# A convolution and feed-forward kernel: the conv one unit later in its block, and the softmax of a batch in four pieces

## The chip, the cores and the metric

The kernel runs on one core of one Trainium2 chip. The metric is device time in microseconds (us), from start to end of the program on that core. A core has several engines that run side by side and wait for each other by semaphores: TensorE (PE in the profile, with its weight loads shown as PEld), VectorE (DVE), ScalarE (ACT), GpSimd (POOL), and SyncE (SP), which here only issues DMA transfers.

## What is computed

Two stages follow each other. The first is a convolution whose weights come from a softmax: for each of 8 batches, 4096 positions and 8 heads, 7 numbers are turned into weights, and these weigh the last 7 positions of `x`. The second is a feed-forward layer with a squared ReLU on each of the 32768 positions.

```python
# x: (8, 4096, 192), weight_gen: (8, 4096, 8, 7), w_in: (192, 2048), w_out: (2048, 192)
w = np.exp(weight_gen - max over the 7)
w = w / (sum over the 7 + 1e-09)
x_pad = six zero rows ahead of x in each batch
out[b, s, h] = sum over k of w[b, s, h, k] * x_pad[b, s + k, h]      # 24 channels a head
h = np.maximum(out.reshape(32768, 192) @ w_in, 0.0)
result = (h * h) @ w_out
```

## The kernel before

The work is cut into 33 blocks. Blocks 0 and 1 hold 512 positions each, all others two sub-blocks of 512. A batch is 8 sub-blocks, so batch 3 begins with block 13 and each later batch four blocks after the one before it.

In each block the program issues 16 units (`u`, the first product with `w_in`), eight half quarters (`M`, the second product of the block before), and one conv (`C`), which makes the input of the next block. Softmax pieces are put in ahead of chosen units. The order from block 7 on:

```python
steady_spread = "MuMuuu" * 2 + "MCuMuuu" + "MuMuuu"
```

A unit: three pairs of matmuls into an `h` buffer of PSUM (a pool of three, which the conv shares), a ReLU on ACT into `t1`, and for two units together the square on DVE into `g`.

```python
def st_unit(j, u):
    h = ps_h.tile([P, 2, TB], f32, name="h", tag="h")     # ps_h: 3 buffers
    ...        # three pairs of 64-row matmuls, 512 columns: L518
    nc.scalar.activation(out=t1[:, e], in_=h, func=ActF.Relu)             # L532
    ...
    nc.vector.tensor_tensor(out=g[...], in0=t1[...], in1=t1[...], op=AluOp.mult)   # L536
```

A quarter of the second product is two half quarters: the first needs `g` of units 0 to 7 of the block before, the second that of units 8 to 15. Its result is summed by ACT and DVE.

```python
def quarters():
    ...
        st_mm2(j, qt, FCS[0], (0, 1), o)      # 32 matmuls, 64 rows, 192 columns: L560
        yield
        st_mm2(j, qt, FCS[1], (0, 1), o)
        o_sum(j, qt, (0, 1), o)               # ACT copy L574, then DVE add L576
        ...
        yield
```

The conv reads two bands, one for each sub-block, that DVE makes in the same block ahead of units 1 and 5 from the softmax weights. Its matmuls alternate between the two sub-blocks. The first two columns of heads are done into one `h` buffer, the other two into a second; ACT casts the first and DVE the second.

```python
def st_band(j, tiles):
    nc.vector.tensor_tensor(out=bd_t[j][...], in0=wr_t[j][...], in1=mask[...], op=AluOp.mult)  # L381

def st_conv_spread(j):
    for ks in ((NK, NK - 1), (0, 1)):
        yp = ps_h.tile([P, 2, TB], f32, name="yp", tag="h")
        for k in ks:
            for i in range(NT):
                for half in (0, 1):           # the two sub-blocks
                    for e in (0, 1):
                        nc.tensor.matmul(out=yp[p0 : p0 + 32, k - k0, a:b],
                                         lhsT=x_t[s][...], rhs=bd[...], ...)       # L450
        copy = nc.vector.tensor_copy if k0 == 0 else nc.scalar.copy
        copy(out=y[:, k0 : k0 + 2], in_=yp)                                        # L460
    ...        # four DMA moves inside y, from SyncE
```

The softmax of a batch works on 32 rows a partition and 6 of halo (batch 2: two parts of 16 and 6). A piece is a range of these rows: the exponential on ACT, then, at its place in the plan, on DVE a sum, a reciprocal, and products into `v_big`, four to each run of rows inside a group of 8. After the last piece the weights go to DRAM, and from there the rows of each sub-block are loaded for its band.

```python
def soft(s):
    lo, hi = next(s.softs)
    s.total(lo, hi)                    # DVE reduction L257
    s.recip(lo, hi)                    # DVE reciprocal L264
    s.scale(lo, hi, nc.vector)         # DVE products L272, four per run of rows
    if hi < s.rh:
        return
    ...
        s.store(nc.sync)               # vd<-v_big, L286
        stored.add(s)
        for w in [w for w in waiting if w[0] is s]:
            waiting.remove(w)
            load_rows(w[1])            # wr<-vd, lines 323 to 333
```

For each block j the program calls `load_rows(j + 2)` at the start; if the store has not been issued by then, the loads are issued right behind it.

```python
PIECE = 8
TIMES = {
    ...
    (2, 1): ((7, 9), (7, 13), (8, 9)),                       # (block, unit) of each piece
    (3, 0): ((9, 9), (9, 13), (10, 9), (10, 13), (11, 0)),
}
...
times = TIMES.get((b, k)) or (
    (f - 6, 9), (f - 5, 9), (f - 4, 9), (f - 3, 9), (f - 3, 13)   # f: the batch's first block
)
```

Of the kernel before, what the change touches and what calls it, by code (L numbers as in the profile page):

```python
# [9 lines left out]
def kernel(  # L10
# [49 lines left out]
    R = S // P  # L60
    HALO = KK - 1
# [37 lines left out]
    FIRST = 8  # L99
# [495 lines left out]
    with nc.allow_low_precision("fp16 matmul pipeline"), tc.manual_schedule():  # L595

        block_of = {n: j for j, (s, c) in enumerate(BLOCKS) for n in range(s, s + c)}
        parts = []
# [65 lines left out]


        steady = "MuMuuu" * 3 + "MuuuMCu"
        steady_spread = "MuMuuu" * 2 + "MCuMuuu" + "MuMuuu"
        plans = {
            0: "B1 X1 u u u E1 S1 u C u u u u",
            1: "L3 u u B2 M E2 B3 u M E2 u u S2 u M u C u S2 M",  # L670
# [8 lines left out]
        def at(j, u, kind, *args):  # L679
            fill.setdefault((j, u), []).append((kind, *args))  # L680

        PIECE = 8

        TIMES = {
            (1, 0): ((3, 15), (4, 0)),
            (1, 1): ((4, 15), (5, 0)),
            (1, 2): ((4, 2), (5, 1), (5, 15)),
            (2, 0): ((6, 1), (6, 15), (7, 0)),
            (2, 1): ((7, 9), (7, 13), (8, 9)),
            (3, 0): ((9, 9), (9, 13), (10, 9), (10, 13), (11, 0)),  # L690
        }

        def exp_time(j, u):

            if u == 0:
                return j - 1, 12
            return j, {1: 0, 2: 1, 7: 3, 8: 4, 9: 4, 13: 12, 15: 8}[u]

        for n, s in enumerate(parts):
            piece = s.rh if n < 2 else PIECE  # L700
            s.pieces = [(lo, min(lo + piece, s.rh)) for lo in range(0, s.rh, piece)]
            s.exps = iter(s.pieces)
            s.softs = iter(s.pieces)
        for n, s in enumerate(parts[4:], 4):
            b, f = s.b, s.fb
            k = n - min(m for m, p in enumerate(parts) if p.b == b)
            times = TIMES.get((b, k)) or (
                (f - 6, 9), (f - 5, 9), (f - 4, 9), (f - 3, 9), (f - 3, 13)
            )
            assert len(times) == len(s.pieces)  # L710
            for j, u in times:
                at(*exp_time(j, u), "E", n)
                at(j, u, "S", n)
            at(times[0][0] - 1, 0, "L", n)
# [65 lines left out]
        for j in range(NBLK):  # L780
# [3 lines left out]
            for step in plans[j].split():  # L784
                kind, n = step[0], int(step[1:] or 0)
# [73 lines left out]
```

## Time and profile before

| | us |
|---|---|
| median of 3 runs | 743.38 |
| lowest and highest | 742.02, 743.45 |
| span of the profiled execution | 740.5 |
| TensorE busy | 730.4 |
| DVE busy | 626.1 |
| ACT busy | 617.1 |

"Busy" is the time in which at least one instruction of an engine is shown as running. Matmuls overlap, and the profile works out their ends, so a busy TensorE need not be one at its peak. A line of the timeline has the start, the length, the engine, the line of the kernel, the operation, what it writes and reads, the number of instructions merged into it, and, in brackets, how long the engine was idle before and what ended this. A line of the table of windows has the stretch, its length, the busy time and number of instructions of each engine, the clock granted to TensorE, and the share and rate of the DMA engines. The largest groups by line of the kernel, with busy time in us and the mean of one in ns:

```profile
L532 ACT ACTIVATE t<-h 128x1024 f16<-128x1024 f32 x512 | 496.2, 1025 | 53.3 <-PE h L518 52.9
...
L536 DVE TENSOR_TENSOR g<-t 128x2048 f16<-128x2048 f16 (+1 forms) x309 | 308.5, 1036 | 26.9 <-ACT t L532 26.6
...
L381 DVE TENSOR_TENSOR bd<-wr,mask 128x4160 f16<-128x4160 f16 (+3 forms) x89 | 149.3, 1702 | 4.9 <-DMA wr<-v_first 4.9
```

### The profile page before, as it was taken

To read this page: it belongs to the slowest core of one execution; us is meant where nothing else is said; L and a number is where in the kernel's file an instruction comes from. 1 tells how busy PE (TensorE), PEld (TensorE's weight loads), DVE (VectorE), ACT (ScalarE), POOL (GpSimd) and SP (SyncE) were. 2 spreads that over 40 slices of the span, in tenths; PEclk is the share of its full clock that TensorE was granted. 3 is DMA by queue.
4 is the path that set the end of the run, shared out by engine and by line. 5 is a ranking of instruction groups with operands and counts; after the bars stand their busy time and mean duration, and the time that the engine had idled before them with its cause. 6 is when DMAs were issued, how large, how long until landed. Compare 5 with 4: busy or idle time off the path is not lost. (4 is left out here: it accounts for less than half of the span.)

```text
span 740.5 us, 31100 instructions
## 1 busy us (share of the span) xinstructions
PE 730.4 (99%) x14106; PEld 531.9 (72%) x14106; DVE 626.1 (85%) x824; ACT 617.1 (83%) x730; POOL 100.1 (14%) x148
## 2 busy tenths in 40 slices
PE   7999999999999999999999999999999999999998
PEld 3767777877777777777777777777777777777777
DVE  4999898999899988889888889889889887778853
ACT  4998888988888888888888888888888888888883
POOL 7322222321001100011000110010100110001000
PEclk9999999999999999999999999999999999999999
DMA  7845444794454432545335444353444334444012
GB/s 206 131 82 135 80 68 106 145 156 116 96 126 77 93 74 66 123 105 95 56 69 130 92 86 81 62 126 100 65 87 80 62 85 81 66 86 76 29 45 66
DMA packets 126544, 68.71 MB, mean 93 GB/s; under 512 B 85193, under 2 KB 122636, under 8 KB 125900
## 3 DMA queue, kind: packets, MB, share of 16 engines
q1 hardware_dynamic: 80908, 48.12, 22.8%
q0 software_dynamic: 45360, 18.50, 21.5%
q8 instruction: 110, 1.80, 1.0%
q14 instruction: 22, 0.18, 0.1%
q10 hardware_dynamic: 144, 0.10, 0.0%
HBM read 50.18 MB, written 28.70 MB: 107 GB/s over the span
## 5 line engine op out<-in xcount | busy, mean ns | idle before, releaser
L532 ACT ACTIVATE t<-h 128x1024 f16<-128x1024 f32 x512 | 496.2, 1025 | 53.3 <-PE h L518 52.9
L560 PEld LDWEIGHTS <-g 64*128 64x128 f16 (+1 forms) x8032 | 344.3, 94 | 62.8 <-DVE g L536 3.5
L560 PE MATMUL o<-w_o,g 64*128 64x192 f16 (+1 forms) x8032 | 380.7, 243 | 1.1 <-DVE g L536 0.8
L536 DVE TENSOR_TENSOR g<-t 128x2048 f16<-128x2048 f16 (+1 forms) x309 | 308.5, 1036 | 26.9 <-ACT t L532 26.6
L518 PE MATMUL h<-y,w_p 64*128 64x512 f16 x2400 | 291.9, 376 | 0.0
L518 PEld LDWEIGHTS <-w_p 64*128 64x128 f16 x2400 | 112.7, 94 | 96.4
L381 DVE TENSOR_TENSOR bd<-wr,mask 128x4160 f16<-128x4160 f16 (+3 forms) x89 | 149.3, 1702 | 4.9 <-DMA wr<-v_first 4.9
L576 DVE TENSOR_TENSOR o_sb<-o,o_sb 128x384 f32<-128x384 f32 x123 | 68.4, 556 | 68.8 <-ACT o_sb L574 68.1
L333 POOL DMA_DIRECT2D xt<-in_x_dram x62 | 52.1, 844 | 426.8 <-PE yp L450 366.7
L574 ACT COPY o_sb<-o 128x384 f32<-128x384 f32 x129 | 61.5, 477 | 44.3 <-PE o L560 44.3
L518 PE MATMUL h<-y,w_i 64*128 64x512 f16 (+1 forms) x768 | 82.2, 350 | 1.8 <-ACT t L532 0.8
L518 PEld LDWEIGHTS <-w_i 64*128 64x128 f16 x768 | 37.2, 94 | 27.7 <-issue 4.0
L460 ACT CAST y<-yp 128x1024 f16<-128x1024 f32 x25 | 25.3, 1012 | 12.3 <-PE yp L450 12.3
L450 PE MATMUL yp<-bd,xt 128*32 128x104 f16 (+1 forms) x2000 | 31.8, 210 | 0.1
L460 DVE CAST y<-yp 128x1024 f16<-128x1024 f32 x25 | 30.4, 1216 | 0.0
L450 PEld LDWEIGHTS <-xt 128*32 128x32 f16 x2000 | 26.1, 95 | 5.9 <-issue 4.2
L272 DVE TENSOR_TENSOR v_big<-ex,rcp 128x112 f16<-128x112 f32 (+1 forms) x136 | 27.3, 263 | 2.5 <-DMA vd<-v_big 1.3
L250 ACT ACTIVATE ex<-wg 128x448 f32<-128x448 f32 (+2 forms) x44 | 27.0, 617 | 1.8 <-DMA wg<-in_weight_gen_dram 1.8
L257 DVE TENSOR_REDUCE ssum<-ex 128x64 f32<-128x448 f32 (+2 forms) x44 | 26.1, 594 | 2.3 <-ACT ex L250 2.3
L264 DVE RECIPROCAL rcp<-ssum 128x64 f32<-128x64 f32 (+2 forms) x44 | 23.7, 539 | 1.5
L323 POOL DMA_DIRECT2D xt<-in_x_dram x7 | 3.9, 553 | 126.2 <-PE yp L450 90.3
L363 POOL DMA_DIRECT2D wr<-v_first x31 | 16.9, 564 | 16.0 <-DVE v_first L272 15.8
(34 smaller groups left out, 95.4 us busy)
## 6 DMA issues: line engine op xcount, KB each, us to landing
out_dram<-o_sb SPq DMA_DIRECT2D x63, 384.0 KB
xt<-in_x_dram POOLq DMA_DIRECT2D x42, 240.0 KB, 4.7
wg<-in_weight_gen_dram SPq DMA_DIRECT2D x4, 1064.0 KB
xt<-in_x_dram POOLq DMA_DIRECT2D x20, 192.0 KB, 4.9
wr<-vd SPq DMA_DIRECT2D x38, 80.0 KB
vd<-v_big SPq DMA_DIRECT2D x5, 512.0 KB
y<-y SPq DMA_DIRECT2D x100, 24.0 KB
wg<-in_weight_gen_dram SPq DMA_DIRECT2D x5, 392.0 KB
```

The lines of the kernel that those rows point to most:

```text
L250: nc.scalar.activation(out=self.ex[:, lo:hi].rearrange("p r g k e -> p (r g) k e"), in_=self.wg[:, lo:hi].rearrange("p r (g e) k -> p (r g ...
L272: eng.tensor_tensor(out=bass.AP(tensor=v.tensor, offset=v.offset + lo * H * SL + lo % SL * 2 + g * SL * 2, ap=[list(v.ap[0]), [H * SL + 2, ...
L333: eng.dma_start(out=dst[:, first:last], in_=ap)
L381: nc.vector.tensor_tensor(out=bd_t[j][:, H * lo : H * (lo + len(tiles) * n)].rearrange("p (g m c) -> p g m c", g=shape[1], c=2 * SL), in0= ...
L450: nc.tensor.matmul(out=yp[p0 : p0 + 32, k - k0, a:b], lhsT=x_t[s][:, i, c0 : c0 + 32], rhs=bd[:, head // 2, e, 0 : b - a], start=True, sto ...
L460: copy(out=y[:, k0 : k0 + 2], in_=yp)
L518: nc.tensor.matmul(out=h[:, half, jj * th : (jj + 1) * th], lhsT=w_in_chunk(w, u * per + jj, slot, half), rhs=y_t[j][r0 : r0 + RT, k, 0:th ...
L532: nc.scalar.activation(out=t1[:, e], in_=h, func=ActF.Relu)
L536: nc.vector.tensor_tensor(out=g[:, a : e + 1], in0=t1[:, a : e + 1], in1=t1[:, a : e + 1], op=AluOp.mult)
L560: nc.tensor.matmul(out=oo[:, cc * Dm : (cc + 1) * Dm], lhsT=g[r0 : r0 + n, cc * P : (cc + 1) * P], rhs=w_o[r0 : r0 + n, fc, :], start=(fc ...
L574: nc.scalar.copy(out=o_sb, in_=o[0][:, c])
L576: nc.vector.tensor_tensor(out=o_sb, in0=o[1][:, c], in1=o_sb, op=AluOp.add)
```

## The change

It has two parts. In the plan of blocks 7 and later the conv moves behind unit 8; its bands, its inputs and its results stay as they are. And the softmax of a batch of 32 rows is cut into four pieces (8, 10, 10 and 10 rows) instead of five (8, 8, 8, 8 and 6). From batch 4 on these stand one to a block, in the blocks 5, 4, 3 and 2 ahead of the batch's first one, where before they stood in the blocks 6 to 3 ahead with two in the last. Batch 3 is handled alike except for its first two pieces, which still share block 9, and the second part of batch 2 has two pieces of 11 rows instead of three. What it is for: the band has more time to be ready ahead of the conv, and DVE and ACT have no block with two pieces of softmax.

```diff
-        steady_spread = "MuMuuu" * 2 + "MCuMuuu" + "MuMuuu"
+        steady_spread = "MuMuuu" * 2 + "MuCMuuu" + "MuMuuu"
...
-        PIECE = 8
+        CUTS = {FIRST: (0, 8, FIRST + HALO), R // 2: (0, 8, 16, R // 2 + HALO), R: (0, 8, 18, 28, R + HALO)}
+        CUTS_FOR = {(2, 1): (0, 11, R // 2 + HALO)}
...
-            (2, 1): ((7, 9), (7, 13), (8, 9)),
-            (3, 0): ((9, 9), (9, 13), (10, 9), (10, 13), (11, 0)),
+            (2, 1): ((7, 9), (8, 9)),
+            (3, 0): ((9, 9), (9, 13), (10, 9), (11, 9)),
...
-            piece = s.rh if n < 2 else PIECE
-            s.pieces = [(lo, min(lo + piece, s.rh)) for lo in range(0, s.rh, piece)]
+            k = n - min(m for m, p in enumerate(parts) if p.b == s.b)
+            cuts = (0, s.rh) if n < 2 else CUTS_FOR.get((s.b, k), CUTS[s.r])
+            s.pieces = list(zip(cuts, cuts[1:]))
...
-                (f - 6, 9), (f - 5, 9), (f - 4, 9), (f - 3, 9), (f - 3, 13)
+                (f - 5, 9), (f - 4, 9), (f - 3, 9), (f - 2, 9)
```

## The prediction

> **What bounds the kernel now.** I read the page first, then the weight loads in order of time, then DVE and SyncE around one conv. The page's busy line:
>
> ```profile
> PE 730.4 (99%) x14106; PEld 531.9 (72%) x14106; DVE 626.1 (85%) x824; ACT 617.1 (83%) x730; POOL 100.1 (14%) x148
> ...
> PEclk9999999999999999999999999999999999999999
> ```
>
> TensorE is hardly ever idle and its clock is never cut, so time falls only where its stream pauses. From block 7 on the stream is periodic, and each block holds one conv. The time from one conv's first weight load to the next, cut into windows with DVE's busy time:
>
> ```profile
> 203.67:226.36 22.69, 20.83 (x29) 1.00 0.52 119
> 226.36:249.20 22.84, 21.84 (x36) 1.00 0.42 88
> ...
> 316.19:338.70 22.51, 20.45 (x30) 1.00 0.44 95
> 338.70:360.82 22.12, 19.17 (x24) 1.00 0.40 72
> 360.82:383.11 22.29, 19.07 (x23) 1.00 0.39 71
> ```
>
> The second number is the length. I call 22.11 us the clean period. Most blocks take 22.27, those with two softmax pieces 22.5 to 22.8. There are two pauses to explain.
>
> Pause one, inside the conv. The weight loads of two convs, each cut off about 0.31 us after its first load:
>
> ```profile
> 316.19 0.41 PEld L450 LDWEIGHTS <-xt 128*32 128x32 f16 x17 [0.16 <-issue]
> ```
>
> ```profile
> 695.23 0.40 PEld L450 LDWEIGHTS <-xt 128*32 128x32 f16 x29 [0.16 <-issue]
> ```
>
> 17 loads against 29 in the same time. In the first, the third of 80 matmuls starts 0.19 us after the first; it is the first to read the band of the second sub-block, and DVE ends that band late:
>
> ```profile
> 314.01 2.31 DVE L381 TENSOR_TENSOR bd<-wr,mask 128x4160 f16<-128x4160 f16 x1
> ```
>
> It ends at 316.32, 0.14 us after the conv's first load. So an ordinary conv's loads take 1.15 to 1.19 us, an undisturbed one's 0.99 to 1.02. The latter come where the last sub-block of a batch is next: its band is cut in two and only the last matmuls need the second part. Of the 25 convs of this form 7 are undisturbed, 17 lose 0.16 us, and one (at 249.20, after a softmax piece at the top of the block) takes 1.34 us and loses 0.35.
>
> Pause two, at the top of the block after one with two pieces:
>
> ```profile
> 329.94 0.11 PEld L560 LDWEIGHTS <-g 64*128 64x128 f16 x4 [0.30 <-DVE g L536]
> ```
>
> The second softmax piece, ahead of unit 13, makes DVE late with the last squares (g), which the second half quarter of the next block needs.
>
> **What the Trainium skill says.** "Perfetto Trace Analysis", Tensor Engine Instruction: the profile's end of a matmul is computed, not observed. The trace agrees: L560 has a mean of 243 ns, but its pairs start 83 ns apart. I therefore count starts. "TensorE: Matmul & The Clock Gate", The mechanism: a weight load passes running matmuls only if its row group differs. Agrees: before a conv, whose loads take all 128 rows, the load queue idles 0.16 us. "VectorE: DVE Perf Modes", The TRN2 errata: a fixed cost for each instruction. Agrees: L272 starts every 207 ns at 112 elements (4 in 0.83 us) and every 178 ns at 84 (4 in 0.71), so 1.07 ns an element and 88 ns fixed. "DMA: Bandwidth & Descriptors", Anatomy of one DMA: the fixed share, mostly completion, is about 2 us. No run here separates it; below I use measured times from store to load.
>
> **Part one: the conv one unit later.** Nothing is added or removed; M, C, u8, M becomes M, u8, C, M. In starts of first matmuls, before: M to conv 1.42 us, conv to u8 1.24 (1.09 undisturbed), u8 to M 0.66, M to u9 1.32: 4.64, or 4.48 undisturbed. After: M to u8 1.32 (as elsewhere, 306.28 to 307.60). From a 512-column unit to a conv there is one pair in the early part, 53.59 to 54.34, so 0.75. Conv to M 1.09, M to u9 1.32. Sum 4.48. So the order itself costs nothing, and the gain is the wait for the band: the conv now starts about 0.65 us later, 0.5 us after the band has ended. 17 x 0.16 + 0.35 = 3.1 us.
>
> Buffers: three h buffers rotate. After the change u9 takes u8's, u10 the first conv half's, u11 the second's. DVE's cast of the second half ends at 319.74 as now (DVE is busy until 318.5 anyway). u10, which needs it today, starts near 319.95; u11, which will, near 320.5. That slack grows.
>
> **Part two: four pieces.** Per batch of 32 rows plus halo, DVE loses one reduction and one reciprocal; with cuts off the multiples of 8, 20 products become 28 shorter ones. From the groups by form: a reduction of 448 elements 609 ns, of 336 493, so 1.04 ns an element; a reciprocal of 64 552, of 48 453, so 6.2 ns each. A 10-row piece: reduction 0.73 + reciprocal 0.65 + four products of 8 rows 0.83 + four of 2 rows 4 x (88 + 28 x 1.07 ns) = 0.47, about 2.6 us with gaps, against 2.0 for 8 rows. Four pieces 9.8 us, five today 9.7 (four of 2.0 and a last of 1.65). DVE's sum stays; its spread changes: one piece a block. What goes:
> - Batches 4 to 7: the piece at unit 13 in blocks 14, 18, 22, 26. 22.52 - 22.27 = 0.25 each, 1.0 us.
> - Block 7: from the window 158.72 to 181.41, 22.69, whose conv is undisturbed: 22.69 - 22.11 = 0.58 gone.
> - Block 10: 22.84 - 22.27 = 0.57 gone.
> - Block 9 keeps both its pieces, and the second grows from 8 to 10 rows. Its excess is 22.69 - 22.11 = 0.58 and should grow by about 0.5.
> Sum 1.0 + 0.58 + 0.57 - 0.5 = 1.6 us.
>
> Do longer pieces at unit 9 delay anything? After an 8-row piece DVE idles 0.42 us before the next o_sum, and TensorE writes that bank again 0.67 us after the sum's end at 325.91. So 0.6 us more delays the sum 0.2 and TensorE not at all; even the 11-row pieces of batch 2 (0.85 more) use up less than this.
>
> **Part three: the later store.** The last piece moves from block f-3, unit 13, to f-2, unit 9, so the chain store, load, band gets short:
>
> ```profile
> SPq L323 <- DMA vd<-v_big: 20.9, 6, 5.8
> ```
>
> ```profile
> 327.58 0.35 SPq L286 DMA_DIRECT2D vd<-v_big  x1
> 332.62 0.33 SPq L323 DMA_DIRECT2D wr<-vd  x1
> 333.00 0.98 SPq L333 DMA_DIRECT2D wr<-vd  x2
> ```
>
> From store to first load 5.0 us here, 2.65 at the shortest (416.77 to 419.42); the loads' packets run until 335.4, 2.8 us more. After the change, put into this block's time, the piece ends near 323.2, the store goes at 323.3, the loads at 326 to 328.3 and land at 329 to 331.1. The band that reads them is now at 331.30 (308.78 + 22.3 gives 331.1). It just fits; an unlucky store makes DVE late by some tenths. Five batches, at 0.1 us each: +0.4.
>
> **Sum.** 743.4 - 3.1 - 1.6 + 0.4 = 739.1 us.
>
> **Rivals.**
> - The conv after a unit costs more. For it: in the early part the load queue idles 0.42 us before such a conv, against 0.16 after a half quarter. Times 25 the difference is 6.5 us: 745. Against it: the load queue runs ahead of the matmuls there, and starts of matmuls show 0.75 from unit to conv, of which the unit takes 0.66. I give it one in ten.
> - The late load becomes the wait. For it: the 5.0 us above and one wait of 5.8. A band late by 1 us eats DVE's slack, then delays o_sum and the second band; I put half a microsecond of it on TensorE, for 5 batches 2.5 us: 741 to 742. Against it: three of the stores took under 3 us. Two in ten.
> - DVE was the hidden bound and takes back what the conv gives. DVE's 19.1 us in a period of 22.1 speaks against it, as do its idle times before o_sum. It would leave 742 to 743. One in ten.
>
> **Range and chances.** Everything that this change can move is the sum of the pauses, about 6 us after block 7, 0.8% of the time. So 2% either way (14.9 us) is out of reach unless something new waits in every block. Low end 736.8: all pauses gone, and block 9 no worse. High end 742: half the gain lost to late loads. Chances: same 0.98, 0.01 each for faster and slower.
>
> **What would show it.** The conv's weight loads at 0.99 to 1.02 us in all 25; periods of 22.10 to 22.15, except one near 23.2 after block 9; no wait of L560 for g at the tops of blocks 8, 11, 15, 19, 23 and 27; about 5 DVE waits for wr from vd, if any, each below 0.5 us. I am wrong on part one if the loads become short but the periods stay at 22.27, and on part three if L381 idles by a microsecond for DMA.

## The result and the profile after

| | before | after |
|---|---|---|
| median, us | 741.74 | 736.27 |
| lowest and highest | 740.44, 743.45 | 735.19, 737.00 |
| span of the profiled execution | 740.5 | 734.8 |

The ratio of after to before is 0.9921, with a 95% interval of 0.9904 to 0.9937: 0.8% faster, or some 5.9 us by the ratio and 5.5 by the medians. The prediction said 739.1 us, with 736.8 as its low end, so the kernel came out 0.5 us below the whole range. The median of before stands 1.6 us below the 743.38 that the prediction started from.

The page's busy line after the change:

```profile
PE 725.9 (99%) x14106; PEld 529.4 (72%) x14106; DVE 627.3 (85%) x856; ACT 613.5 (83%) x724; POOL 100.2 (14%) x148
```

It looks like the old one: TensorE at 99%, DVE at 85%. A reader who stops at shares of busy time sees no difference between the kernels; the difference is in TensorE's pauses, and those show in the time from one conv to the next. The table of windows after the change, with DVE's busy time:

```profile
203.10:226.38 23.28, 21.45 (x33) 1.00 0.37 69
226.38:248.46 22.08, 19.59 (x28) 1.00 0.49 114
314.71:336.80 22.09, 19.59 (x28) 1.00 0.48 115
336.80:358.89 22.09, 19.69 (x28) 1.00 0.50 104
358.89:380.97 22.08, 19.08 (x23) 1.00 0.40 73
```

All 24 periods from the conv in block 7 to the one in block 31 now take 22.07 to 22.12 us, but for the first line here, which holds the second half of block 9 and the top of block 10. From the first of these convs to the last it was 536.5 us before (158.72 to 695.23) and is 531.3 now (158.93 to 690.24): 5.2 us gained. The spans differ by 5.7 us. The other 0.5 us lie ahead of block 7, where nothing on TensorE was changed (taken up at the end); to see it one must count from the half quarter ahead of the first conv, since the conv itself now stands 0.65 us later in its block.

One conv of the kernel after, cut off about 0.31 us after its first weight load:

```profile
314.71 0.40 PEld L450 LDWEIGHTS <-xt 128*32 128x32 f16 x30 [0.42 <-issue]
```

30 loads in the time in which 17 were done before. The instructions around the same conv:

```profile
311.89 2.32 DVE L381 TENSOR_TENSOR bd<-wr,mask 128x4160 f16<-128x4160 f16 x1
...
312.65 1.48 PE L560 MATMUL o<-w_o,g 64*128 64x192 f16 x32
...
313.97 0.81 PE L518 MATMUL h<-y,w_p 64*128 64x512 f16 x6
...
314.71 0.98 PEld L450 LDWEIGHTS <-xt 128*32 128x32 f16 x80 [0.42 <-issue]
```

The band ends at 314.21, 0.50 us ahead of the conv. The load queue's idle time ahead of a conv has grown from 0.16 to 0.42 us, and the conv nevertheless costs no more: from M at 312.65 over u8 at 313.97, the conv at 314.71 and the next M at 315.77 to u9 at 317.10 it takes 4.45 us in starts of matmuls, where the prediction worked out 4.48 and the kernel before took 4.64.

The pause that is left, at the top of block 10, in three parts:

```profile
215.76 0.28 PEld L560 LDWEIGHTS <-g 64*128 64x128 f16 x8 [0.54 <-DVE g L536]
216.37 0.12 PEld L560 LDWEIGHTS <-g 64*128 64x128 f16 x4 [0.32 <-DVE g L536]
216.97 0.11 PEld L560 LDWEIGHTS <-g 64*128 64x128 f16 x4 [0.49 <-DVE g L536]
```

No other block from 7 to 32 waits for g; one wait at 723.3, behind the last block, was there before too (728.9). And the store, its loads, and the bands that read them, for the batch that begins with block 17 (SyncE's lines, then DVE's):

```profile
343.08 0.34 SPq L286 DMA_DIRECT2D vd<-v_big  x1
346.09 0.34 SPq L323 DMA_DIRECT2D wr<-vd  x1
346.48 0.97 SPq L333 DMA_DIRECT2D wr<-vd  x2
```

```profile
350.37 0.56 DVE L576 TENSOR_TENSOR o_sb<-o,o_sb 128x384 f32<-128x384 f32 x1 [1.51 <-ACT o_sb L574]
350.84 2.38 DVE L381 TENSOR_TENSOR bd<-wr,mask 128x832 f16<-128x832 f16 x2
```

The bands start with no idle time before them, 3.4 us after the last load was issued. From store to first load it takes 3.0 us here, and 3.0 to 3.8 for the five batches.

### The profile page after: what moved, and what is told of

It reads as the page before. It is cut to its first block, busy times and chain, and to the rows that moved or that the text cites. A ratio compares the mean times of both kernels' runs of the same rounds, so it can differ in the third digit from the quotient of the medians.

```text
span 734.8 us, 31124 instructions
## 1 busy us (share of the span) xinstructions
PE 725.9 (99%) x14106; PEld 529.4 (72%) x14106; DVE 627.3 (85%) x856; ACT 613.5 (83%) x724; POOL 100.2 (14%) x148
## 4 chain that ended last, share of the span: by engine, by line
PE 70%; DVE 0%; ACT 0%; issue 0%
PE o L560 35%; PE h L518 32%; PE yp L450 3%; DVE g L536 0%; ACT o_sb L574 0%
## 5 line engine op out<-in xcount | busy, mean ns | idle before, releaser
L450 PEld LDWEIGHTS <-xt 128*32 128x32 f16 x2000 | 24.4, 95 | 10.6 <-issue 10.6
L272 DVE TENSOR_TENSOR v_big<-ex,rcp 128x112 f16<-128x112 f32 (+5 forms) x180 | 29.9, 237 | 2.1 <-DMA vd<-v_big 1.1
L450 PE MATMUL yp<-bd,xt 128*32 128x104 f16 (+1 forms) x2000 | 28.3, 209 | 0.0
L250 ACT ACTIVATE ex<-wg 128x560 f32<-128x560 f32 (+4 forms) x38 | 25.9, 682 | 1.7 <-DMA wg<-in_weight_gen_dram 1.7
L257 DVE TENSOR_REDUCE ssum<-ex 128x80 f32<-128x560 f32 (+4 forms) x38 | 25.3, 666 | 2.2 <-ACT ex L250 2.2
L264 DVE RECIPROCAL rcp<-ssum 128x80 f32<-128x80 f32 (+4 forms) x38 | 22.8, 600 | 1.3
```

Source lines behind the costliest of these rows:

```text
L250: nc.scalar.activation(out=self.ex[:, lo:hi].rearrange("p r g k e -> p (r g) k e"), in_=self.wg[:, lo:hi].rearrange("p r (g e) k -> p (r g ...
L272: eng.tensor_tensor(out=bass.AP(tensor=v.tensor, offset=v.offset + lo * H * SL + lo % SL * 2 + g * SL * 2, ap=[list(v.ap[0]), [H * SL + 2, ...
L450: nc.tensor.matmul(out=yp[p0 : p0 + 32, k - k0, a:b], lhsT=x_t[s][:, i, c0 : c0 + 32], rhs=bd[:, head // 2, e, 0 : b - a], start=True, sto ...
```

## The experiments

**The conv alone.**

```diff
-        steady_spread = "MuMuuu" * 2 + "MCuMuuu" + "MuMuuu"      # kernel before
+        steady_spread = "MuMuuu" * 2 + "MuCMuuu" + "MuMuuu"
```

> Only the conv moved behind unit 8; softmax pieces as before. Theory (conv waits for the second band): the 25 convs' weight loads all take 0.96 to 1.00 us, ordinary periods fall from 22.27 to 22.09, and the pauses at the tops of blocks 8, 10, 11, 15, 19, 23 and 27 stay: 17 x 0.18 + 0.35 + 7 x 0.02 = 3.5 us less than before, 738.2 us against 741.7. Rival (the gain of the change is the softmax's, one piece a block, and the conv's place only matters together with it): less than 1 us gained, 740.8 or more.

Measured: 738.36 us against 741.63, ratio 0.9952 (0.9940 to 0.9965). The loads of all 25 convs take 0.96 to 1.00 us; ordinary periods are 22.07 to 22.11; the periods that had a pause of the second kind keep it, at 22.66, 22.69, 22.67 and four of 22.33 to 22.36. Such a pause, at the top of block 15:

```profile
328.62 0.11 PEld L560 LDWEIGHTS <-g 64*128 64x128 f16 x4 [0.30 <-DVE g L536]
```

From the first conv to the last it takes 532.9 us, 3.6 less than before. The theory holds, and its rival, that the conv's place matters only together with the softmax, does not.

**The softmax alone.**

```diff
-        steady_spread = "MuMuuu" * 2 + "MuCMuuu" + "MuMuuu"      # kernel after
+        steady_spread = "MuMuuu" * 2 + "MCuMuuu" + "MuMuuu"
```

> Only the softmax in four pieces; the conv stays ahead of unit 8. Theory: the pauses at the tops of blocks 8, 11, 15, 19, 23 and 27 go (0.58 + 0.57 + 4 x 0.25 = 2.15 us), the one at the top of block 10 grows by 0.6 us, ordinary periods stay at 22.27: 1.6 us less than before, 740.1 us against 741.7. Rival (softmax is the main part): 3 us or more gained, 738.7 or less.

Measured: 739.44 us, ratio 0.9972 (0.9961 to 0.9983), 2.2 us less than before. Ordinary periods stay at 22.25 to 22.30, the third matmul of 17 convs still starts 0.19 us after the first, the period after the conv of block 9 grows to 23.30, and the other pauses for g are gone. From the first conv to the last it takes 534.6 us, 1.9 less than before. Against this the sum of 1.6 was 0.3 us too small for one reason: the conv at 249.20, which lost 0.35 us to the band, lost it because a softmax piece stood at the top of that block. Taking the piece away mends it too (its loads take 1.00 us), so either part alone brings the 0.35 that the prediction put under the conv.

The two gains, 0.48% and 0.28%, add up to 0.76%, with that 0.35 us in both; the change as a whole brings 0.79%. Each of the three is known to some 0.1 to 0.2%, so the parts do not need each other.

**The band in two operations, the conv where it was.**

```diff
         last = NT - int(tile_start(j, NT - 1) != starts[-1])     # kernel before
+        if j % 2 and j >= BLOCKS[FIRST_SPREAD][0]:
+            last = NT - 1
```

> The kernel before, conv and softmax untouched, but the second band of each block from 8 on is made in two operations (tiles 0 to 3, then tile 4), as it is already at the end of a batch; 18 DVE operations more. Theory (the conv's third matmul waits for the second band): the first part ends about 0.4 us earlier, the conv's loads take 0.99 to 1.02 us everywhere, and the time falls by 17 x 0.16 + 0.35 = 3.0 us, to about 738.7, without moving the conv. Rival (the conv's move gains by more slack in the three h buffers and in the casts): nothing gained, 741.7.

Measured: 739.26 us, ratio 0.9971 (0.9960 to 0.9983): 2.4 us gained of the 3.0 expected. It is 17 operations more, not 18: of the 25 convs eight, the one at 249.20 among them, had the second band in two operations already. Nothing in this kernel is moved on TensorE, and still the wait nearly goes:

```profile
312.74 2.38 DVE L381 TENSOR_TENSOR bd<-wr,mask 128x3328 f16<-128x3328 f16 x2
```

```profile
314.91 0.39 PEld L450 LDWEIGHTS <-xt 128*32 128x32 f16 x26 [0.16 <-issue]
```

26 loads in the first 0.31 us instead of 17. What is missing against 30 is the second part of the band, which ends at 315.12, 0.21 us into the conv; the ordinary convs' loads take 1.02 to 1.05 us and their periods 22.13 to 22.17. The conv at 249.20 of before is not helped (1.36 us here): the edit leaves its band as it was. That explains the shortfall: the 17 ordinary convs gain 0.13 us each, 2.2 in all. The rival, slack in the h buffers and the casts, would have left 741.7.

**The second band later, the conv in its new place.**

```diff
             if j + 1 >= FIRST_SPREAD:                             # kernel after
-                us = (1, 5)
+                us = (1, 6)
```

> The changed kernel with the second band ahead of unit 6 instead of unit 5 in blocks 7 and later; nothing else. DVE then makes a pair of squares (1.2 us) ahead of the band, so the band ends 1.2 us later, 0.7 us after the conv's first load instead of 0.5 us ahead of it. Theory: the wait comes back, 0.7 us in 18 convs and 0.5 in the 7 whose band is in two parts, 16 us in all: 752 us against 736.3. Rival: the time stays within 1 us of 736.3.

Measured: 770.55 us, ratio to before 1.0394 (1.0377 to 1.0411). The wait came back as the theory says, but at twice the size. DVE and the conv's loads:

```profile
320.84 0.56 DVE L576 TENSOR_TENSOR o_sb<-o,o_sb 128x384 f32<-128x384 f32 x1 [0.17 <-ACT o_sb L574]
322.04 1.23 DVE L536 TENSOR_TENSOR g<-t 128x2048 f16<-128x2048 f16 x1 [0.64 <-ACT t L532]
323.18 2.32 DVE L381 TENSOR_TENSOR bd<-wr,mask 128x4160 f16<-128x4160 f16 x1
```

```profile
324.13 0.10 PEld L450 LDWEIGHTS <-xt 128*32 128x32 f16 x3 [0.42 <-issue]
325.56 0.96 PEld L450 LDWEIGHTS <-xt 128*32 128x32 f16 x77 [1.33 <-issue]
```

Three loads, then 1.33 us of nothing, then the other 77: the first matmul on the second sub-block holds up all that follow. The profile puts 25 waits of TensorE, 26.4 us together, down to the band. The expectation counted the squares' 1.2 us that now precede the band, but not the 0.64 us for which DVE must first wait for ACT's ReLU, which the squares read; the old order hid that wait under the band. In figures: the ordinary convs' loads take 2.38 us against 0.97, the eight with a cut band 2.23, so 17 x 1.41 + 8 x 1.26 = 34.1 us, and the kernel is 34.3 us slower than the changed one. Here the size of the wait sets the time one for one.

**Two pieces in a block, or one ahead of unit 13.** Two variants of the changed kernel, run beside a repeat of it that serves as their base and as that of the experiment after them:

> The changed kernel once more, as a base on the same chip for the three runs beside it: 736.3 us, periods of 22.09 but for one of 23.28.

Measured: 736.23 us, ratio to before 0.9924 (0.9912 to 0.9937).

```diff
-                (f - 5, 9), (f - 4, 9), (f - 3, 9), (f - 2, 9)    # kernel after
+                (f - 5, 9), (f - 4, 9), (f - 3, 9), (f - 3, 13)   # two_in_block
+                (f - 5, 9), (f - 4, 9), (f - 3, 13), (f - 2, 9)   # one_at_13
```

> The changed kernel, but for batches 4 to 7 the fourth piece stands ahead of unit 13 of block f-3, together with the third, as the old plan had it; the pieces keep 10 rows. Theory (a piece ahead of unit 13 makes the last squares late by what exceeds the slack): four pauses like the one left in the changed kernel, 1.2 us each, so 4.8 us more, 741.1 us. Rival (fewer pieces are what helped, wherever they stand): 736.3 us.

Measured: 741.37 us, ratio to before 1.0001 (0.9991 to 1.0010).

> The changed kernel, but for batches 4 to 7 the third piece stands ahead of unit 13 of block f-3 instead of unit 9; still one piece to a block. Theory that the place ahead of unit 13 makes the pause: the same four pauses of about 1.2 us as with two pieces, 741.1 us. Theory that two pieces in one block are too much for DVE, as the change's purpose says: no pause, 736.3 us.

Measured: 741.01 us, ratio to before 1.0002 (0.9993 to 1.0011).

Both are back at the time of before, though for another reason: the conv's gain stays (its loads take 0.96 to 1.01 us), and four new pauses cost as much as the whole change brings. There are four periods of 23.36 to 23.39 us in the first, of 23.27 to 23.31 in the second, all others at 22.07 to 22.12 except the one after block 9. So two pieces in one block are not what hurts: a single piece is enough, if it stands ahead of unit 13. DVE in one such block of the second variant, and TensorE at the top of the next:

```profile
323.15 0.56 DVE L576 TENSOR_TENSOR o_sb<-o,o_sb 128x384 f32<-128x384 f32 x1 [0.97 <-ACT o_sb L574]
323.62 0.73 DVE L257 TENSOR_REDUCE ssum<-ex 128x80 f32<-128x560 f32 x1
324.38 0.65 DVE L264 RECIPROCAL rcp<-ssum 128x80 f32<-128x80 f32 x1
325.07 1.22 DVE L272 TENSOR_TENSOR v_big<-ex,rcp 128x84 f16<-128x84 f32 x8
326.21 2.42 DVE L536 TENSOR_TENSOR g<-t 128x2048 f16<-128x2048 f16 x3
```

```profile
327.48 0.28 PEld L560 LDWEIGHTS <-g 64*128 64x128 f16 x8 [0.54 <-DVE g L536]
```

DVE idles for 0.97 us just before, so it was not overloaded. But behind the piece come the last three square operations of the block, which end at 328.63, and TensorE asks for all of them in the second half quarter of the next block, whose loads began at 326.13. The exponential moves with the piece, but these squares wait for no ReLU of ACT: they follow the piece with no idle time. The piece delays exactly the work with the nearest deadline.

Its length counts too. Ahead of unit 13, six rows (1.65 us of DVE in the trace of before) lengthen the period by 0.26 us in the kernel with the conv alone, eight rows (1.98 us) by 0.57 to 0.60, and ten rows (2.59 us) by 1.2 here. Each time that is the DVE time less about 1.4 us: an estimate, from these three sizes, of the slack that this place has.

**Batch 3 without a piece ahead of unit 13.**

```diff
-        CUTS_FOR = {(2, 1): (0, 11, R // 2 + HALO)}               # kernel after
+        CUTS_FOR = {(2, 1): (0, 11, R // 2 + HALO), (3, 0): (0, 12, 24, R + HALO)}
...
-            (3, 0): ((9, 9), (9, 13), (10, 9), (11, 9)),
+            (3, 0): ((9, 9), (10, 9), (11, 9)),
```

> The changed kernel, but batch 3 has three pieces (12, 12 and 14 rows), ahead of unit 9 of blocks 9, 10 and 11, and none ahead of unit 13. Worked out as in the prediction these take DVE 3.0, 3.0 and 3.35 us, 1.0 to 1.35 more than a piece of 8 rows; the slack after unit 9 is 0.42 + 0.67 = 1.09 us, so only the last one makes TensorE wait, 0.3 us, and the pause of 1.2 us at the top of block 10 goes: 0.9 us gained, 735.4 us. Rival (pieces of this size at unit 9 cost as much as one at unit 13): 736.3 us or more.

Measured: 734.68 us, ratio to before 0.9911 (0.9898 to 0.9924), the best of all. The interval overlaps that of the changed kernel beside it (0.9912 to 0.9937), so the trace has to tell whether the gain is real. Its windows:

```profile
202.13:224.21 22.08, 19.95 (x27) 1.00 0.39 72
224.21:246.29 22.08, 19.93 (x28) 1.00 0.50 114
246.29:268.49 22.20, 20.30 (x28) 1.00 0.50 103
```

The period of 23.28 is gone, and from first to last conv it takes 530.2 us against 531.4 in the repeated changed kernel: 1.2 us gained. The cost of the longest piece, 14 rows, is where it was expected, but the period there grows by 0.11 us (22.20) instead of 0.3:

```profile
253.11 2.35 DVE L536 TENSOR_TENSOR g<-t 128x2048 f16<-128x2048 f16 x2
255.38 0.55 DVE L576 TENSOR_TENSOR o_sb<-o,o_sb 128x384 f32<-128x384 f32 x1
```

```profile
255.98 1.25 PEld L560 LDWEIGHTS <-g 64*128 64x128 f16 x30 [0.26 <-issue]
```

DVE has no idle time left before o_sum, the sum ends at 255.93, and TensorE's loads go on at 255.98 after a pause of 0.26 us. The profile names no cause for that pause; that TensorE waits there for the bank that o_sum frees fits the times, but is not shown. The periods with the two pieces of 12 rows stay at 22.08.

## Why the prediction was off, step by step

- **Conv, the wait for the band:** right. Predicted 3.1 us; the conv alone brings 3.6 us from first to last conv (532.9 against 536.5). The term that was too small is the clean period: 22.11 us was read from convs whose band is cut in two, and these still lose about 0.02 us, which fits the second part of the band: it ends 0.18 us after the conv's first load. Without it the period is 22.09, which over 24 periods makes the missing 0.5 us.
- **Conv, the order of work on TensorE:** right. The count by starts of matmuls gave 4.48 us, the trace 4.45. The first rival, built on the load queue's idle time, is refuted: that idle time did grow, by 0.26 us in each of 25 convs, and cost nothing. So is the third, that DVE takes back what the conv gives: DVE's busy time is 1.2 us longer, and all but one period are at 22.07 to 22.12.
- **Four pieces:** right in the places of the pauses, and in size but for one conv. Predicted 1.6 us, with block 9 about 0.5 worse; measured 1.9 from first to last conv (534.6 against 536.5), with block 9 worse by 0.6, and with the 0.35 us of one conv that the prediction had counted under the other part. No piece at unit 9 of the changed kernel delays TensorE, and DVE's sum stays (627.3 against 626.1 us). The fixed cost of 88 ns for a product was misread: it came from the length of four products together divided by four. Their starts lie 186 ns apart at 112 elements and 156 at 84, so 1.07 ns an element stands, but the fixed share is 66 ns. The ten-row piece took 2.58 us all the same, where 2.6 was worked out. The prediction laid the pause to the second piece of a block, ahead of unit 13; the place alone is enough, as a block with one piece there showed.
- **The later store:** a step that failed. "Five batches, at 0.1 us each: +0.4" should be zero: in the whole trace no wait of DVE is put down to the loads of `wr` from `vd`. The prediction took 2.7 to 5.0 us from store to load and found that it "just fits"; it took 3.0 to 3.8, and the band shown above began 3.4 us behind the last load. The second rival is refuted with it. (In the repeat of the changed kernel one idle time of 1.5 us ahead of an o_sum bears the name of these loads. That place is idle for as long in other blocks, as the 1.51 us above show, and the period there is 22.07.)
- **The sum:** its start is the step that failed by most. 743.4 was the median of three executions that lay high (742.02, 743.38, 743.45); with three more it is 741.7, and 12 and 35 executions beside the later runs give 741.6 and 741.2. Of the 2.8 us between 739.1 and 736.3 this start makes 1.6, the clean period 0.5 and the loads that were never late 0.4; the last 0.3 are what the medians (5.5 us) show beyond the periods (5.2 us). The effect, put at 4.3 us, was right in its mechanism and 0.9 us too small by the periods. From 741.7 even the predicted effect ends at 737.4, inside the range. The low end, 6.6 us below the start, would have been 735.1 from there: it allowed for "all pauses gone" but for no scatter of the start.

What stays open is the half microsecond between 5.2 us by the periods and 5.7 by the spans. It lies ahead of block 7: the half quarter before the first conv of block 7 began at 157.31 us before and at 156.88 after. In the kernel with the cut band, whose program up to there is that of before, it began at 156.49, and in the repeat of the changed kernel at 156.45. So it is within what two executions of one program differ by; what makes them differ is not known.

## What to carry to other kernels

With TensorE at 99% in both kernels, the period of its pattern, held against a block that lacks the pause, showed what a new order could bring. A late result cost time where its consumer came next in the queue; moving the consumer back by one piece of independent work, or cutting the producer so that its first part suffices, took the wait away. Extra work on a helper engine belongs ahead of results with a far deadline: the same ten-row softmax piece cost nothing ahead of unit 9 and 1.2 us ahead of unit 13, with DVE busy for 627 us in both kernels.

## What was not expected of the hardware

A 0.42 us gap in the weight-load queue ahead of each conv that follows a 512-column unit went with no loss on the matmul side. In starts of matmuls, u8 to conv is 0.74 us, 0.08 more than a unit ahead of an M takes (0.66); but M to conv took 1.42 before, 0.10 more than M to a unit (1.32), with an idle time of only 0.16 us. In this kernel idle time on that queue alone is not a measure of lost time.
